# Scores of the first batch's chunks two ahead, with four unread products per chunk

## The chip, the cores and the metric

The kernel runs on one core of a Trainium2 chip. A core has five engines with instruction queues of their own that run in order: TensorE (PE, matrix products), VectorE (DVE), ScalarE (ACT), GpSimd (POOL) and SyncE (SP), which here issues nearly all DMA. The metric is device microseconds of one execution, given as the median of several; lower is better.

## The reference, cut to what matters

There are 4 batches, 8 heads, 768 tokens and a head size of 48. The first part is a recurrence with a complex decay in each of the 48 rows of a state of 48 x 48 per head:

```
a = (a_re, a_im) * min(|a|, 0.999) / (|a| + 1e-6)
for t in range(768):
    S = a[t][:, None] * S + outer(k[t], v[t])      # complex S
    y[t] = q[t] @ real(S)
```

Its output, as 768 x 384 per batch, goes through a Fourier transform over tokens and one over features, of which the real part is added to it (u = x + mixed), a normalisation, an MLP of 384 -> 1536 -> 384, a token mixing MLP of 768 -> 256 -> 768 and a second MLP, each added to its input. The weights come as 64-bit floats.

## The kernel before, in words

For each batch the program has a scan on DVE (line 312 for the first batch, 540 for the others), which makes decayed queries and keys for every token; a chunk stage (lines 739 to 832), in which the 768 tokens are worked in 8 chunks of 96; the Fourier stage with the normalisation (`stage2`, line 954); and the dense products (`mlp`, `tok1`, `tok2`). The dense part of a batch runs beside the scan of the next, but the first batch has nothing dense to run beside, so its scan, chunk stage and Fourier stage stand at the program's start, up to about 192 us.

A chunk c in the first batch:

- `ch_load(c)` has SP load V (line 741) and the decayed keys Kn (line 744); two buffers of each, so chunk c+2 loads when chunk c has been read.
- `ch_sc(c, half)` makes the scores of 4 heads (line 753, TensorE, four products into one of three PSUM buffers "s"), and DVE multiplies them with the causal mask (line 760) into SBUF.
- `ch_u(c)` makes the chunk's own state u(c) = keys x values (lines 768 and 769, 16 small products into a PSUM buffer "l", of which there are three). DVE adds the state T(c-1) that came in, giving Aa(c) (line 779), and multiplies by the chunk's decay: lines 785 and 786 on DVE, 787 on POOL (in chunk 0 on DVE), and their sum is T(c) (line 789). Each chunk needs the T of the chunk before.
- `ch_y(c)` adds two products in PSUM, masked scores x values (line 802) and queries x T(c-1) (line 808); ACT copies the sum to xT (line 810).

Between the chunks the first batch converts the 64-bit weights to pairs of 32-bit parts (`convert`, lines 180 to 207): SP loads a tile (line 185), ACT runs lines 191 and 192, DVE line 194, POOL line 196, DVE line 199, ACT line 205, POOL line 206, and SP writes the parts to memory (line 207). `tick` advances the tiles that are under way by one step per chunk and begins as many new ones as the table `CF` says.

`warm(n, x)` (line 305) issues n products into a fresh "l" buffer that nobody reads. `WC` (line 32) says how many follow each y(c) of the first batch: 10 after chunk 6 and 12 after chunk 7.

After the chunks, `stage2` adds and subtracts pieces of xT: lines 982 and 988, for s = 0 on DVE and for s = 1 on POOL in the first batch, then line 999 on DVE, products with the transform's matrices (lines 1022 and 1033), their sums and differences cb on POOL (lines 1070 and 1071), and line 1085 on DVE, which adds them to the input.

The order on each engine is worked out by a scheduler when the program is built, from priorities in program order and from its own timing of the program; so a changed program order changes the order of every queue in places.

Of the kernel before, what the change touches and what calls it, by code (L numbers as in the profile page):

```python
# [28 lines left out]
W0, WS = 2, 8  # L29
CF = (2, 2, 2, 2, 2, 0, 8, 0)  # L30
AN = (5, 6, 6, None)
WC = (0, 0, 0, 0, 0, 0, 10, 12)
WZ, CL = 0, 1
XL = (0,), (0, 1, 2, 3, 4, 5)
AH = 4
# [18 lines left out]
def attn_fft_mixer_kernel(ctx: ExitStack, tc: tile.TileContext, aL, xL, vL, wL, qN, kN, vN, arN, aiN,  # L54
# [37 lines left out]
    def alloc(tag, shape, dt=F32, name=None):  # L92
        n = 1
        for x in shape[1:]:
            n *= x
        t = pool.tile([128, SIZE[tag]], dt, tag=tag, bufs=BUFS[tag], name=name or tag)
        return shaped(t[0:shape[0], 0:n], shape)
# [3 lines left out]
    def palloc(tag, shape):  # L101
        n = 1
        for s in shape[1:]:
            n *= s
        t = psum.tile([128, 512], F32, tag=tag, bufs=PSB[tag], name=tag)
        v = t[0:shape[0], 0:n]
        if len(shape) == 3:
            v = v.rearrange("p (a b) -> p a b", b=shape[2])
        return v
# [120 lines left out]
    def tick(n, loads=False):  # L230

        keep, stream[0] = stream[0], BACK
        active[:] = [g for g in active if next(g, "end") != "end"]
        for _ in range(n):
            g = begin()
            next(g)
            if not loads:
                next(g)
            active.append(g)
        stream[0] = keep  # L240
# [64 lines left out]
    def warm(n, x):  # L305

        ps = palloc("l", [128, 512])
        for _ in range(n):
            te.matmul(out=ps[:, 0:x.shape[1]], lhsT=ident[0:x.shape[0], :], rhs=x)
# [391 lines left out]
    def stage1(b):  # L701
# [34 lines left out]
        st = {}  # L736
        PU = "l" if b == 0 else "s"

        def ch_load(c):
            v = alloc("P", [96, 384], name="V")  # L740
            sp.dma_start(out=v, in_=vL[b, c])
            kt = alloc("A", [96, 8, 128], name="Kn")
            for hf in range(2):
                sp.dma_start(out=kt[48 * hf:48 * hf + 48],
                             in_=knd[hf].rearrange("(h c) s f -> c s h f", c=8)[c])
            st[c] = dict(v=v, kt=kt)

        def ch_sc(c, half):
            ps = palloc("s", [96, 4, 96])
            Q, K = qk[0][:, 1], qk[0][:, 0]  # L750
            for j in range(4):
                hc = (half * 4 + j) * 8 + c
                te.matmul(out=ps[:, j, :], lhsT=K[:, hc, :], rhs=Q[:, hc, :])  # L753
            sc = alloc("e", [96, 4, 96], name="sc")
            mb = mask.unsqueeze(1).to_broadcast([96, 4, 96])
            if half and OFF[2] & (1 << b):
                se.copy(out=sc, in_=ps)
                ge.tensor_tensor(out=sc, in0=sc, in1=mb, op=ALU.mult)
            else:
                ve.tensor_tensor(out=sc, in0=ps, in1=mb, op=ALU.mult)  # L760
            st[c][f"sc{half}"] = sc

        def ch_u(c):
            d = st[c]
            ps = palloc(PU, [112, 8, 48])
            for h in range(8):
                vv = d["v"][:, h * 48:h * 48 + 48]
                te.matmul(out=ps[0:64, h, :], lhsT=d["kt"][:, h, 0:64], rhs=vv)  # L768
                te.matmul(out=ps[64:112, h, :], lhsT=d["kt"][:, h, 64:112], rhs=vv)
            g = gm[b % 2].rearrange("p k (h c) -> p k h c", c=8)[:, :, :, c:c + 1]  # L770

            def gb(k, lo, hi):
                return g[lo:hi, k].to_broadcast([hi - lo, 8, 48])

            def v8(ap):
                return ap.rearrange("p (h e) -> p h e", e=48)
            if c:
                a = alloc("e", [112, 384], name="Aa")
                ve.tensor_tensor(out=v8(a), in0=v8(st["T"]), in1=ps, op=ALU.add)  # L779
                a = v8(a)  # L780
            else:
                a = ps
            y = yc[c % 2]
            x = alloc("e", [112, 384], name="Xx")
            ve.tensor_tensor(out=v8(x), in0=a, in1=gb(0, 0, 112), op=ALU.mult)
            (ge if c and b else ve).tensor_tensor(out=v8(y)[0:48], in0=a[64:112], in1=gb(1, 64, 112), op=ALU.mult)  # L786
            st["yop"] = (ge if c else ve).tensor_tensor(out=v8(y)[64:112], in0=a[0:48], in1=gb(1, 0, 48), op=ALU.mult)
            T = alloc("e", [112, 384], name="T")
            st["op"] = ve.tensor_tensor(out=T, in0=x, in1=y, op=ALU.add)
            st["Tn"] = T  # L790
            if b == 0:
                tops.append(st["op"])

        def ch_y(c):
            d = st[c]
            Q = qk[0][:, 1]
            ps = palloc(PU, [112, 4, 96])
            for p in range(4):
                for k in range(2):
                    h = 2 * p + k  # L800
                    m = 48 if k else 64
                    te.matmul(out=ps[64 * k:64 * k + m, p, :], lhsT=d["v"][:, h * 48:h * 48 + m],  # L802
                              rhs=d[f"sc{h // 4}"][:, h % 4, :], start=True, stop=(c == 0))
                if c:
                    for k in range(2):
                        h = 2 * p + k
                        m = 48 if k else 64
                        te.matmul(out=ps[64 * k:64 * k + m, p, :], lhsT=st["T"][:, h * 48:h * 48 + m],  # L808
                                  rhs=Q[:, h * 8 + c, :], start=False, stop=True)
            marked(se.activation(out=xT[:, :, c * 96:c * 96 + 96], in_=ps, func=ACTF.Copy, scale=gate[0:112, b:b + 1]))  # L810

        if b == 0:
            tick(CF[0])
        st_g2()
        ch_load(0)
        ch_load(1)
        ch_sc(0, 0)
        ch_sc(0, 1)
        for c in range(8):
            if c < 7:  # L820
                ch_u(c)
                ch_sc(c + 1, 0)
                ch_sc(c + 1, 1)
            ch_y(c)
            if b == 0 and WC[c]:
                warm(WC[c], ident)
            st["T"] = st.get("Tn")
            if c < 6:
                ch_load(c + 2)
            if b == 0 and c < 7:  # L830
                rests[0], rests[1] = tops[c], st["yop"]
                tick(CF[c + 1], c == 5)
# [366 lines left out]
    def chain(b):  # L1199
        stage1(b)  # L1200
        return stage2(b)
# [145 lines left out]
```

## Time and profile before

| what | us |
|---|---|
| median of 3 runs | 1102.39 |
| lowest and highest run | 1101.18, 1103.57 |
| the profiled execution | 1103.4 |
| its span on the core | 1101.6 |
| TensorE busy | 985.5 (89%) |
| VectorE busy | 784.3 (71%) |
| ScalarE busy | 506.2 (46%) |
| GpSimd busy | 387.3 (35%) |

The shares are means over the whole span. The granted clock of TensorE has a mean of 0.955 of full speed. Where a row gives a matrix product of 32-bit floats, it counts two records per product: "x8" is four products.

### The profile page before, as it was taken

Reading aid. Unit: us, or ns where it says so; the run is one execution under the profiler, and the core shown is the slowest. Engines: PE = TensorE matmul, PEld = TensorE weight load, DVE = VectorE, ACT = ScalarE, POOL = GpSimd, SP = SyncE. Lnnn points to the kernel's source line nnn. Section 1 sums busy time; section 2 is a strip of 40 time slices with the busy share of each in tenths; the row PEclk is TensorE's granted clock in tenths of the full one; section 3 lists DMA queues with packets and bytes.
Section 4 is the critical chain, followed back from the end, with each engine's and each line's share of the span. In section 5 each row is a group of like instructions: output and inputs, shape, how many; then the busy total and the mean of one; then the engine's idle time right before and its main releaser. Section 6 shows DMA issues by size and latency. Waiting matters only on the chain.

```text
span 1101.6 us, 21033 instructions
## 1 busy us (share of the span) xinstructions
PE 985.5 (89%) x7314; PEld 923.1 (84%) x7314; DVE 784.3 (71%) x2115; ACT 506.2 (46%) x1393; POOL 387.3 (35%) x520
## 2 busy tenths in 40 slices
PE   1368887999889999799998999999986999999997
PEld 0237775989788888699998899999976999999997
DVE  6986987999999668999767879985555433433332
ACT  6753355777876225867423567751124112121111
POOL 6643985573576444223226312211432002000000
PEclk9987797999999998899998999999988999999999
DMA  6137954686758664355565336655412433443432
GB/s 215 45 82 179 293 176 154 209 283 194 231 179 278 194 178 135 99 168 185 179 160 172 112 112 193 205 161 146 139 48 66 151 115 129 158 151 130 165 101 74
DMA packets 101536, 174.65 MB, mean 159 GB/s; under 512 B 11056, under 2 KB 61104, under 8 KB 100912
## 3 DMA queue, kind: packets, MB, share of 16 engines
q1 hardware_dynamic: 101424, 173.24, 51.1%
q8 instruction: 60, 0.98, 0.4%
q14 instruction: 52, 0.43, 0.1%
HBM read 133.88 MB, written 39.32 MB: 157 GB/s over the span
## 4 chain that ended last, share of the span: by engine, by line
PE 65%; DVE 10%; DMA 2%; ACT 1%; issue 1%; POOL 1%; SPq 0%; POOLq 0%; DVEq 0%; ACTq 0%
PE l L942 24%; PE l L926 22%; PE s L753 3%; PE s L642 2%; PE s L1033 2%; PE s L1022 2%; PE s L802 2%; DMA cvt<-wL 2%; PE s L808 1%; PE s L1147 1%; DVE ws L982 1%; PE s L1165 1%; PE s L768 1%; DVE cvt L199 1%; PE s L906 1%
## 5 line engine op out<-in xcount | busy, mean ns | idle before, releaser
L942 PE MATMUL l<-w,h 128*128 128x384 f32 x1728 | 332.5, 345 | 12.1 <-DVE h L932 8.4
L926 PE MATMUL l<-th,w 128*128 128x384 f32 x1152 | 314.4, 342 | 5.1 <-DVE h L932 2.6
L942 PEld LDWEIGHTS l<-w,h 128*128 128x128 f32 x1728 | 304.4, 192 | 16.8 <-DVE h L932 11.6
L926 PEld LDWEIGHTS l<-th,w 128*128 128x128 f32 x1152 | 210.8, 190 | 9.1 <-DVE h L932 4.1
L930 ACT ACTIVATE h<-l 128x384 fp32r<-128x384 f32 x192 | 94.0, 490 | 225.3 <-PE l L926 224.8
L926 PE MATMUL l<-tl,w 128*128 128x384 f32 x576 | 195.3, 339 | 0.0
L932 DVE SCALAR_TENSOR_TENSOR h<-l,h 128x384 fp32r<-128x384 f32 x192 | 106.2, 553 | 88.3 <-ACT h L930 87.9
L945 DVE TENSOR_TENSOR u<-u,l 128x384 f32<-128x384 f32 x192 | 105.4, 550 | 76.0 <-PE l L942 75.1
L926 PEld LDWEIGHTS l<-tl,w 128*128 128x128 f32 x576 | 109.1, 189 | 0.4 <-issue 0.2
L196 POOL TENSOR_TENSOR cvt<-cvt 128x384 int32<-128x384 int32 x56 | 64.8, 1163 | 38.2 <-DVE cvt L194 9.4
L466 PE MATMUL s<-misc,y 128*112 128x128 f32 x96 | 22.1, 377 | 52.1 <-DVE y L444 48.6
L753 PE MATMUL s<-qkt 112*96 112x96 f32 x512 | 59.7, 267 | 8.0 <-DVE sc L760 7.9
L466 PEld LDWEIGHTS s<-misc,y 128*112 128x112 f32 x96 | 14.5, 181 | 61.9 <-issue 27.3
L753 PEld LDWEIGHTS s<-qkt 112*96 112x96 f32 x512 | 53.4, 177 | 11.1 <-DVE sc L760 8.7
L786 POOL TENSOR_TENSOR yc<-Aa,gm 48x384 f32<-48x384 f32 x18 | 21.0, 1165 | 100.8 <-DVE Aa L779 100.8
L206 POOL TENSOR_TENSOR w<-cvt,w 128x384 fp32r<-128x384 f32 x44 | 51.1, 1170 | 10.5 <-ACT w L205 7.0
L199 DVE SCALAR_TENSOR_TENSOR cvt<-cvt 128x384 int32<-128x384 int32 x56 | 48.8, 878 | 7.0 <-POOL cvt L196 6.8
L1132 POOL TENSOR_TENSOR xl<-u,xh 128x384 fp32r<-128x384 f32 x18 | 17.9, 1004 | 101.1 <-ACT xh L1131 101.1
L571 POOL TENSOR_TENSOR tm<-tm 128x144 f32<-128x144 f32 (+1 forms) x51 | 26.6, 523 | 73.7 <-ACT tm L570 73.7
L642 PE MATMUL s<-misc,y 128*112 128x128 f32 x288 | 45.7, 275 | 1.5 <-DVE y L626 1.0
L615 DVE TENSOR_TENSOR p<-p,A 128x144 f32<-128x144 f32 x144 | 44.7, 310 | 2.0
L589 POOL TENSOR_TENSOR A<-raw,tm 128x144 f32<-128x144 f32 (+1 forms) x51 | 26.1, 513 | 56.0 <-DVE tm L587 29.4
(232 smaller groups left out, 1905.3 us busy)
## 6 DMA issues: line engine op xcount, KB each, us to landing
w<-wscr SPq DMA_DIRECT2D x180, 384.0 KB, 3.5
cvt<-wL SPq DMA_DIRECT2D x56, 384.0 KB, 4.7
wscr<-w SPq DMA_DIRECT2D x44, 384.0 KB, 3.2
Kn<-kn SPq DMA_DIRECT2D x64, 192.0 KB, 3.8
kn<-y SPq DMA_DIRECT2D x96, 96.0 KB, 2.7
raw<-aL SPq DMA_DIRECT2D x48, 144.0 KB, 3.0
xx<-xL SPq DMA_DIRECT2D x48, 144.0 KB, 3.2
V<-vL SPq DMA_DIRECT2D x32, 144.0 KB, 3.3
```

The lines of the kernel that those rows point to most:

```text
L196: x = ge.tensor_tensor(out=a, in0=a, in1=lo, op=ALU.add)
L199: rest(ve.scalar_tensor_tensor(out=a, in0=hi, scalar=-0x80000000, in1=a, op0=ALU.bitwise_and, op1=ALU.bitwise_or))
L206: ge.tensor_tensor(out=parts[:, 1, :], in0=a.bitcast(F32), in1=r32(parts[:, 0, :]), op=ALU.subtract)
L466: te.transpose(ps[:, j, :], y[:, j, 0:112], ident)
L615: ve.tensor_tensor(out=cur, in0=prev, in1=A[:, j, 0:3, :], op=ALU.mult)
L642: te.transpose(ps[:, j, :], y[:, j, 0:112], ident)
L753: te.matmul(out=ps[:, j, :], lhsT=K[:, hc, :], rhs=Q[:, hc, :])
L926: te.matmul(out=ps, lhsT=w1[:, wi, kt * 128:kt * 128 + 128], rhs=x[g][:, kt, :], start=(n == 0), stop=(n == 8))
L930: x = se.activation(out=hi, in_=ps, func=ACTF.Relu)
L932: ve.scalar_tensor_tensor(out=h[:, 1, g * 384:g * 384 + 384], in0=ps, scalar=0.0, in1=r32(hi), op0=ALU.max, op1=ALU.subtract)
L942: te.matmul(out=ps, lhsT=hs[m][:, hi, tt * 128:tt * 128 + 128], rhs=w2[:, wi, :], start=(n == 0), stop=(n == 8))
L945: ve.tensor_tensor(out=u[tt], in0=u[tt], in1=ps, op=ALU.add)
```

## The change

`WC` gets 4 unread products after each of the chunks 0 to 5 of the first batch. The scores of the first batch are made and masked two chunks ahead instead of one: before the loop for chunks 0 and 1, and in round c for chunk c+2. As scores of a chunk can now come before its load, the chunk's dictionary is made by whoever comes first. The other batches stay one chunk ahead. The table of conversions `CF` is as before.

```diff
-WC = (0, 0, 0, 0, 0, 0, 10, 12)
+WC = (4, 4, 4, 4, 4, 4, 10, 12)
...
-            st[c] = dict(v=v, kt=kt)
+            st.setdefault(c, {}).update(v=v, kt=kt)
...
-            st[c][f"sc{half}"] = sc
+            st.setdefault(c, {})[f"sc{half}"] = sc
...
-        ch_sc(0, 0)
-        ch_sc(0, 1)
+        lead_sc = 2 if b == 0 else 1
+        for c in range(lead_sc):
+            ch_sc(c, 0)
+            ch_sc(c, 1)
         for c in range(8):
             if c < 7:
                 ch_u(c)
-                ch_sc(c + 1, 0)
-                ch_sc(c + 1, 1)
+            if c + lead_sc < 8:
+                ch_sc(c + lead_sc, 0)
+                ch_sc(c + lead_sc, 1)
             ch_y(c)
             if b == 0 and WC[c]:
                 warm(WC[c], ident)
```

Lines after 832 carry a number higher by 3 in the changed kernel: 982 is 985 there, 988 is 991, 1070 is 1073.

The first place is TensorE's queue in the middle of u(0), at the start of the chunk stage (lines 768 and 769 are u(0), 753 the scores):

```order
 L769 MATMUL l<-V,Kn 48x48
 L768 MATMUL l<-V,Kn 64x48
-L753 MATMUL s<-qkt 96x96 x4
+L753 MATMUL s<-qkt 96x96 x12
 L769 MATMUL l<-V,Kn 48x48
 L768 MATMUL l<-V,Kn 64x48
```

Where one half of chunk 0's scores stood, both halves of chunk 1 stand as well.

The second place is POOL's queue from the product of chunk 5 to the first sums of the Fourier stage (787 is a chunk's product, 196 and 206 are conversions, 982 and 988 pieces of the Fourier stage, 1070 and 1071 the sums cb). Before:

```order
L787 TENSOR_TENSOR yc_80<-Aa,gm_81 48x384
L196 TENSOR_TENSOR cvt<-cvt 128x384
L206 TENSOR_TENSOR w<-cvt,w 128x384 x2
L196 TENSOR_TENSOR cvt<-cvt 128x384
L982 TENSOR_TENSOR xf<-xT 112x4x96
L206 TENSOR_TENSOR cvt<-cvt 128x384
L787 TENSOR_TENSOR yc_79<-Aa,gm_81 48x384
L988 TENSOR_TENSOR xd<-xf 112x2x96 x2
L206 TENSOR_TENSOR cvt<-cvt 128x384
```

And in the changed kernel:

```order
L787 TENSOR_TENSOR yc_80<-Aa,gm_81 48x384
L196 TENSOR_TENSOR cvt<-cvt 128x384 x2
L985 TENSOR_TENSOR xf<-xT 112x4x96
L206 TENSOR_TENSOR cvt<-cvt 128x384
L991 TENSOR_TENSOR xd<-xf 112x2x96 x2
L206 TENSOR_TENSOR cvt<-cvt 128x384
L787 TENSOR_TENSOR yc_79<-Aa,gm_81 48x384
```

The product of chunk 6 has moved behind the two of line 988 and the conversion that followed it; two conversions of line 206 stand ahead of chunk 5's product now.

The third place is POOL's queue after the last pieces of the Fourier stage's input. Before:

```order
L196 TENSOR_TENSOR cvt<-cvt 128x384 x6
L206 TENSOR_TENSOR cvt<-cvt 128x384 x5
L196 TENSOR_TENSOR cvt<-cvt 128x384
L206 TENSOR_TENSOR cvt<-cvt 128x384
L196 TENSOR_TENSOR cvt<-cvt 128x384
L1070 TENSOR_TENSOR ws<-ws 128x193
```

And in the changed kernel:

```order
L196 TENSOR_TENSOR cvt<-cvt 128x384 x6
L206 TENSOR_TENSOR cvt<-cvt 128x384
L196 TENSOR_TENSOR cvt<-cvt 128x384
L206 TENSOR_TENSOR cvt<-cvt 128x384 x2
L196 TENSOR_TENSOR cvt<-cvt 128x384
L206 TENSOR_TENSOR cvt<-cvt 128x384 x4
L1073 TENSOR_TENSOR ws<-ws 128x193
```

Seven of line 206 stand ahead of the first sum where six stood; the eight of line 196 come earlier among them.

## Rows read from the trace of the kernel before

**Rows 1.** The page: busy us of each engine, and the end chain by engine.
```profile
PE 985.5 (89%) x7314; PEld 923.1 (84%) x7314; DVE 784.3 (71%) x2115; ACT 506.2 (46%) x1393; POOL 387.3 (35%) x520
...
PE 65%; DVE 10%; DMA 2%; ACT 1%; issue 1%; POOL 1%; SPq 0%; POOLq 0%; DVEq 0%; ACTq 0%
```

**Rows 2.** Busy time by stretch: from:to, length, busy of engines, clock, DMA.
```profile
84.00:97.00 13.00, 11.30 (x131) 10.37 (x131) 6.83 (x23) 2.13 (x9) 0.00 (x0) 0.56 0.45 95
97.00:152.00 55.00, 43.32 (x541) 39.00 (x540) 48.90 (x74) 24.20 (x55) 46.53 (x38) 0.83 0.93 285
152.00:170.50 18.50, 17.93 (x130) 15.14 (x128) 13.88 (x18) 8.32 (x21) 18.04 (x16) 0.96 0.33 129
```

**Rows 3.** DVE's timeline, T of chunks 0, 2, 6: start, us, what, idle before.
```profile
94.15 0.56 DVE L789 TENSOR_TENSOR T<-Xx,yc 112x384 f32<-112x384 f32 x1
...
107.28 0.56 DVE L789 TENSOR_TENSOR T<-Xx,yc 112x384 f32<-112x384 f32 x1 [0.74 <-POOL yc L787]
...
138.94 1.18 DVE L789 TENSOR_TENSOR T<-Xx,yc 112x384 f32<-112x384 f32 x1
```

**Rows 4.** DVE's waits from 84 to 152 us: total, times, longest.
```profile
DVE T L789 <- POOL yc L787: 2.5, 2, 1.8
...
DVE Aa L779 <- PE l L769: 0.9, 1, 0.9
```

**Rows 5.** Lines 786, 199 and 206 in the stage: ns minimum/median/maximum.
```profile
L786 DVE TENSOR_TENSOR yc<-Aa,gm x6: 1103/1270/1410, 98.3 to 137.4; 48x384 f32<-48x384 f32 x6
L786 DVE TENSOR_TENSOR yc<-l,gm x1: 559/559/559, 93.0 to 93.0; 48x384 f32<-48x384 f32 x1
...
L199 DVE SCALAR_TENSOR_TENSOR cvt<-cvt x10: 544/548/1361, 102.0 to 135.8; 128x384 int32<-128x384 int32 x10
...
L206 POOL TENSOR_TENSOR w<-cvt,w x8: 997/1310/3370, 104.8 to 130.1; 128x384 fp32r<-128x384 f32 x8
```

**Rows 6.** TensorE's timeline: scores in the opening and later, unread products.
```profile
89.95 1.60 PE L753 MATMUL s<-qkt 112*96 112x96 f32 x8
...
96.99 1.60 PE L753 MATMUL s<-qkt 112*96 112x96 f32 x16
...
141.49 1.61 PE L309 MATMUL l<-misc 128*128 128x128 f32 x12
```

**Rows 7.** Busy time and granted clock (third from the end) in the opening.
```profile
92.00:96.00 4.00, 4.00 (x43) 3.74 (x41) 3.66 (x9) 0.00 (x0) 0.00 (x0) 0.57 0.45 98
96.00:100.00 4.00, 4.00 (x89) 3.85 (x87) 2.84 (x5) 0.58 (x1) 2.12 (x2) 1.00 0.56 153
```

**Rows 8.** Timelines of DVE and POOL where both idle.
```profile
103.39 0.36 DVE L194 TENSOR_SCALAR cvt<-cvt 128x384 int32<-128x384 int32 x1 [0.87 <-ACT cvt L191]
...
104.75 1.38 POOL L206 TENSOR_TENSOR w<-cvt,w 128x384 fp32r<-128x384 f32 x1 [3.13 <-DVE Aa L779]
...
111.78 0.55 DVE L199 SCALAR_TENSOR_TENSOR cvt<-cvt 128x384 int32<-128x384 int32 x1
```

**Rows 9.** Timelines of POOL and DVE at the end of the chunk stage.
```profile
139.67 4.25 POOL L982 TENSOR_TENSOR xf<-xT 112x384 f32<-112x384 f32 x2
...
140.04 1.00 DVE L760 TENSOR_TENSOR sc<-s,misc 96x384 f32<-96x384 f32 x2
...
144.57 0.86 DVE L982 TENSOR_TENSOR xf<-xT 112x384 f32<-112x384 f32 x1 [1.51 <-ACT xT L810]
...
147.72 1.64 POOL L988 TENSOR_TENSOR xd<-xf 112x192 f32<-112x192 f32 x2
```

**Rows 10.** Timelines of POOL and DVE before the Fourier stage's sums.
```profile
167.32 0.99 POOL L206 TENSOR_TENSOR cvt<-cvt 128x384 fp32r<-128x384 f32 x1
...
169.56 0.52 POOL L1070 TENSOR_TENSOR ws<-ws 128x193 f32<-128x193 f32 x1
...
170.42 0.34 DVE L1085 TENSOR_TENSOR u<-s,ws 128x192 f32<-128x192 f32 x1
```

**Rows 11.** The chain that ended last, one of its pieces: start, us, what.
```profile
349.97 7.49 DMA cvt<-wL
```

## The prediction

> **What bounds the kernel now.** I read first the page's busy line and its end chain [rows 1]. Over the span TensorE is the busy engine (89%) and 65% of the chain is TensorE. But most of the span is the dense products, which the change leaves alone; what it does in the chunk stage of the first batch has to be read from that stage.
>
> So second the table by stage [rows 2]. The chunk stage has two parts. From 84 to 97 us POOL is idle, DVE half idle, and TensorE busy for 11.3 of 13 us: the opening is a TensorE stretch. From 97 to 152 us TensorE is busy for 43.3 of 55 us, DVE for 48.9 and POOL for 46.5. From 152 to 170.5 us POOL is busy for 18.0 of 18.5.
>
> Third the DVE timeline at the product T of each chunk (line 789), which the next chunk needs [rows 3]: T starts at 107.28 in chunk 2 and at 138.94 in chunk 6, so four chunks take 31.7 us, 7.9 each. What sets that pace? DVE waits for TensorE once after the opening, 0.9 us at Aa (line 779) of chunk 1, and twice, 2.5 us, for POOL [rows 4]; no later chunk waits for a score product or a y product. Instead the two engines lengthen each other. Line 786 takes 0.56 us in chunk 0, where POOL idles, and a median of 1.27 us in chunks 1 to 6; line 199 takes 0.55 at its shortest and 1.36 at its longest in the stage; line 206 takes 0.99 at 167.32, where DVE idles, and up to 3.37 in the stage [rows 5, 10]. Alone, a chunk's five POOL instructions would be some 5 x 1.0 = 5.0 us and DVE's work on SBUF operands 5 x 0.55 + 2 x 0.36 = 3.5 us; the sum, 8.5, is near the measured 7.9, the larger of the two is not. I therefore treat DVE and POOL as one resource from 97 us until line 1085 at 170.42, and ask when its work starts and how long both users stand idle at once.
>
> The Trainium skill has a rule for it (SBUF — State Buffer, section "SBUF: two separate sides"): DVE with two SBUF inputs and GpSimd take one port pair as an exclusive lock, and the later one blocks for the whole instruction. It speaks against this change, since by it a late start is not made up out of the idle time of either engine. The lengthened rows above agree.
>
> **The change, part by part.**
>
> *Opening.* TensorE's queue has three halves of scores (12 products) between the two parts of u(0) where there was one. At that place a half, 8 records, takes 1.60 us [rows 6], since the granted clock is at its lower level (0.57 over 92 to 96) [rows 7]; so the second part of u(0) comes 3.2 us later, and with it T(0), which started at 94.15. Of this, the scores of chunk 1 were TensorE's work before T(1) anyway. Counted up to the end of u(1), TensorE has this more to do: the scores of chunk 2, 16 records in 1.60 us, which run at the upper level, and four unread products at 1.61/6 = 0.27 each (12 records are 6 products), 1.07 together [rows 6]. The sum is 2.7, less some 0.1 of pipeline overlap, 2.6. Aa(1) waited for u(1) before (0.9 [rows 4]) and will again. DVE alone would be ready a little earlier: T(0) ends at about 97.9, two masks (1.0) and two of line 194 (0.7) follow, 99.6, against u(1) at some 99.7. So the term is **+2.6**. If the clock rose only after all of this, everything at the lower level would cost about 5.2; if it rose early enough to halve the two moved halves, 2.6 − 1.6 = 1.0. I take 2.6, because the rows put the rise at about 95, and TensorE's work before that is the same.
>
> *What the shared stretch absorbs.* Only time in which both engines idle can give the delay back. There is 0.87 us before line 194 at 103.39 (ACT waited for a weight load), about 0.5 until POOL's line 206 at 104.75, while DVE reads PSUM, and some 0.4 until line 199 at 111.78: 1.8 us [rows 8]. POOL's own 3.13 us before 104.75 is mostly DVE's working time. The weight loads that ACT waited for stand in SP's queue behind V, which waits for y(0), so they come later too, by 1.5 us or more. I take **−1.3**, between 0 and −1.8.
>
> *The middle chunks.* Masks and conversions are the same in number. The four unread products cost TensorE 1.07 us per chunk, twice that at the lower clock, and it has 11.7 us free between 97 and 152 [rows 2]. They take a third buffer of the PSUM ring of three, so y(c+1) now waits for ACT's copy of y(c), and u(c+1) for Aa(c). Behind a late y stand V, the next two weight loads and Kn in SP's queue, and behind those u, two chunks on. DVE's and POOL's 7.9 us per chunk cover this, and I cost it at 0; if the cover goes, a wait like the 0.9 us of Aa(1) appears.
>
> *T(6) and the tail.* On POOL the product of chunk 6 (line 787) now stands behind one more of line 206 and two of line 988: 0.99 + 1.64 = 2.6 us [rows 9, 10]. Against it, y(7) no longer waits for two masks behind T(6). T(6) ended at 140.1, and DVE's line 982 of the last piece started at 144.57, having waited 1.51 for ACT's copy of y(7) [rows 3, 9]; with 1.00 of masks and the 1.61 of unread products gone from between, these 4.4 us become about 1.9. The two cancel. Term **0**, from −1.0 (the masks) to +1.7 (POOL's transforms held up by DVE's for longer, as in the 4.25 us of two at 139.67).
>
> *Before cb(0).* POOL has seven of line 206 instead of six between line 982's last piece and line 1070, which releases line 1085: 0.99 us. Line 1085 started 0.34 after line 1070's end (169.56 + 0.52) [rows 10], behind a line 199 that is now earlier, so some 0.3 of it is hidden. Term **+0.7**, from 0 to 1.0.
>
> *After 192 us* the same work follows, with some loads and transposes in another order; cost 0, with a spread (a rival, below).
>
> Sum: +2.6 − 1.3 + 0 + 0.7 = **+2.0 us**. The profiled execution took 1103.4 us, its span of 1101.6 and 1.8 around it; it would take 1105.4. It lies 1.0 above the median of the runs, 1102.39 (1101.18 to 1103.57), so I predict **1104.4 us**. The ends of the terms add up to −1.8 (1.0 − 1.8 − 1.0 + 0) and +7.9 (5.2 + 0 + 1.7 + 1.0).
>
> **Rivals.**
>
> *Faster: DVE's chain sets the end, and the opening is swallowed.* If the two engines do not exclude each other as I read it, POOL's 3.13 us of idle time before 104.75 takes in the whole +2.6, and the end of the stage is DVE's chain, which loses the 1.51 us wait for ACT and the 1.00 of the last two masks: 1102.4 − 2.5 = 1099.9. For it: DVE's waits [rows 4, 9]. Against it: the lengthened rows [rows 5]. It decides if line 982 of the last piece, 144.57 before, starts by 142.1.
>
> *No change: the clock rises earlier.* With more products in a row in the opening, TensorE would reach the upper level sooner. Only the opening gains, since the later chunks do not wait for TensorE: the two moved halves at 0.80 (half of 16 records' 1.60) instead of 1.60, 1.6 less, so the sum is +0.4 and the time 1102.8. Against it: TensorE was already busy for 4.00 of 4 us between 92 and 96, and still at 0.57 [rows 7]. The Trainium skill (TensorE: Matmul & The Clock Gate, "Part 1: The HAM clock gate") has activity release the throttle, which would make this rival likelier.
>
> *The order after 192 us decides.* Weight loads stand on the end chain as pieces, one of 7.49 us [rows 11]. About half of such a piece more or less, 4 us, gives 1100.4 or 1108.4. For it: the orders of all engines differ in places up to the end. Against it: mostly neighbours have changed places.
>
> **How the numbers follow.** No change is what lies within 0.2% of 1102.4, that is 1100.2 to 1104.6, about what a measurement of this kernel can tell. My forecast has a chance of 0.60, with a spread of about 2 us around 1104.4: 0.30 slower, 0.30 no change. DVE's chain: 0.17, of which 0.13 faster and 0.04 no change. Earlier clock: 0.10, of which 0.08 no change and 0.02 slower. The order after 192: 0.13, of which 0.05 faster, 0.02 no change and 0.06 slower. Together 0.18 faster, 0.44 no change, 0.38 slower. The forecast's own range is 1102.0 to 1107.0; with the rivals, 1099.6 to 1107.6 leaves out about 0.2.
>
> **What would show it.** Right: Aa(1) at 99.4 to 100; chunks 2 to 6 still 7.6 us or more apart; line 786 still at a median of 1.27 us; line 1085 about 2 us after 170.42. Wrong: chunks closer than 7.4 us (then TensorE or its clock did count); Aa(1) before 98.5 (the clock); line 1085 at or before 170.4 (absorbed); or a stretch from line 1085 to the end that differs from 1101.6 − 170.4 = 931.2 us by over 2.

## The result, and the profile after

| what | before | after |
|---|---|---|
| median of 4 runs, us | 1102.91 | 1115.89 |
| lowest and highest run | 1101.18, 1103.57 | 1112.32, 1116.53 |
| the profiled execution's span | 1101.6 | 1114.7 |

The ratio is 1.0111 (95%: 1.0095 to 1.0126): slower by 12.2 us, where the forecast was 2.0 and its range ended at 1107.6. Below line 832 every line number of the changed kernel is 3 higher: L985 is line 982 before, L1088 is 1085.

The page of the changed kernel, busy us and the end chain by engine, answers to [rows 1]. TensorE has 3.4 us more work in a span that is 13.1 longer, and the chain leans more on DVE (16% for 10%):

```profile
PE 988.9 (89%) x7362; PEld 924.8 (83%) x7362; DVE 790.8 (71%) x2115; ACT 503.8 (45%) x1393; POOL 383.6 (34%) x520
...
PE 60%; DVE 16%; ACT 2%; issue 2%; POOL 1%; DMA 1%; POOLq 0%; DVEq 0%; ACTq 0%
```

The first batch's start, by stretch as in [rows 2] and [rows 7] (length, busy time of PE, PEld, DVE, ACT, POOL, granted clock, DMA):

```profile
84.00:97.00 13.00, 11.28 (x114) 10.40 (x115) 6.40 (x22) 1.66 (x8) 0.00 (x0) 0.60 0.38 82
97.00:152.00 55.00, 44.55 (x599) 39.08 (x597) 48.96 (x73) 24.58 (x50) 42.97 (x38) 0.91 0.91 276
92.00:96.00 4.00, 4.00 (x43) 3.77 (x42) 2.45 (x6) 0.00 (x0) 0.00 (x0) 0.70 0.05 11
```

DVE's timeline in the chunk stage, for [rows 3], [rows 9] and [rows 10]: start, us, what, idle before. T of chunk 0, Aa(1), T of chunks 2 and 5, two pieces of line 991, Aa(6), T of chunk 6, line 982's last piece, and line 1088, the first to read the Fourier stage's sums:

```profile
96.52 0.56 DVE L789 TENSOR_TENSOR T<-Xx,yc 112x384 f32<-112x384 f32 x1
99.28 0.55 DVE L779 TENSOR_TENSOR Aa<-T,l 112x384 f32<-112x384 f32 x1 [0.73 <-PE l L769]
...
109.16 0.56 DVE L789 TENSOR_TENSOR T<-Xx,yc 112x384 f32<-112x384 f32 x1 [0.74 <-POOL yc L787]
...
131.24 0.56 DVE L789 TENSOR_TENSOR T<-Xx,yc 112x384 f32<-112x384 f32 x1 [0.74 <-POOL yc L787]
...
135.87 3.33 DVE L991 TENSOR_TENSOR xd<-xf 112x192 f32<-112x192 f32 x2
139.12 0.54 DVE L779 TENSOR_TENSOR Aa<-T,l 112x384 f32<-112x384 f32 x1
...
141.48 1.18 DVE L789 TENSOR_TENSOR T<-Xx,yc 112x384 f32<-112x384 f32 x1
...
147.69 0.56 DVE L985 TENSOR_TENSOR xf<-xT 112x384 f32<-112x384 f32 x1 [0.62 <-ACT xT L810]
...
173.40 1.37 DVE L1088 TENSOR_TENSOR u<-s,ws 128x192 f32<-128x192 f32 x4 [3.28 <-POOL ws L1073]
```

Before, T(5) and Aa(6) stood here:

```profile
130.32 1.34 DVE L789 TENSOR_TENSOR T<-Xx,yc 112x384 f32<-112x384 f32 x1
...
133.72 0.54 DVE L779 TENSOR_TENSOR Aa<-T,l 112x384 f32<-112x384 f32 x1
```

T is 2.4 us late in chunk 0 (94.15), 1.9 in chunk 2 (107.28), 2.5 in chunk 6 (138.94); line 982's last piece is 3.1 late, L1088 3.0. From there to the end of the span it takes 1114.7 − 173.4 = 941.3 us, against 931.2 before: 10.1 of the 13.1 us arise after the part that the prediction worked out.

Line 786, which the prediction took as the sign that DVE and POOL lengthen each other, is as before or a little shorter (median 1.18 for 1.27 us) [rows 5]:

```profile
L786 DVE TENSOR_TENSOR yc<-Aa,gm x6: 1101/1180/1280, 100.4 to 140.3; 48x384 f32<-48x384 f32 x6
```

DVE's waits from 84 to 152 us answer to [rows 4]: at T 1.5 us for POOL, 0.7 for TensorE at Aa(1); after 100 us it waits for no product of TensorE at all, but at line 199 it waits 2.3 us for POOL, for 0.4 before:

```profile
DVE T L789 <- POOL yc L787: 1.5, 2, 0.7
...
DVE Aa L779 <- PE l L769: 0.7, 1, 0.7
```

TensorE's timeline answers to [rows 6]: three halves of scores in the opening, then four unread products. Then the piece that the prediction did not see: y(7) with the unread products of chunk 7 (24 records, 12 products) between its first four records and the rest:

```profile
89.97 4.16 PE L753 MATMUL s<-qkt 112*96 112x96 f32 x24
...
97.00 1.16 PE L309 MATMUL l<-misc 128*128 128x128 f32 x8
...
139.72 0.58 PE L802 MATMUL l<-sc,V 96*64 96x96 f32 x4 [4.06 <-DVE Aa L779]
140.23 5.48 PE L309 MATMUL l<-misc 128*128 128x128 f32 x24
145.64 0.38 PE L808 MATMUL l<-qkt,T 112*64 112x96 f32 x4
```

The clock in that stretch (length, busy time of TensorE alone, granted clock, DMA): TensorE is idle for 3.7 of 4 us, then runs at the lower level, and is back at the upper one in the course of the next four:

```profile
136.00:140.00 4.00, 0.28 (x4) 0.84 1.00 321
140.00:144.00 4.00, 4.00 (x21) 0.50 1.02 379
144.00:148.00 4.00, 3.02 (x37) 0.80 0.54 172
```

After 192 us, the busy time of TensorE alone by stretch (length, busy, granted clock, DMA), first before:

```profile
180.00:300.00 120.00, 110.08 (x617) 0.95 0.67 215
300.00:460.00 160.00, 144.55 (x1247) 0.95 0.57 176
...
800.00:860.00 60.00, 48.53 (x274) 0.86 0.22 69
sum 680.00, PE 639.77; mean PE 127.95
```

and after:

```profile
180.00:300.00 120.00, 106.93 (x607) 0.96 0.64 208
300.00:460.00 160.00, 140.87 (x1234) 0.97 0.58 178
...
800.00:860.00 60.00, 45.16 (x297) 0.83 0.14 49
sum 680.00, PE 629.71; mean PE 125.94
```

The sums are of 180 to 860. TensorE's idle time there is 680 − 639.77 = 40.2 us before and 680 − 629.71 = 50.3 after. From 860 to 1060 it is busy throughout in both. So in these two profiles the engine that bounds the dense part waits 10.1 us more, about as much as is lost after L1088. Its longest waits from 192 us to the end, after (total, times, longest):

```profile
PE s L909 <- ACT ws L1115: 14.4, 5, 5.7
PE l L945 <- DVE u L948: 6.2, 5, 2.5
PE s L1025 <- ACT ws L1009: 5.8, 1, 5.8
```

and before:

```profile
PE s L906 <- ACT ws L1112: 12.1, 4, 5.7
...
PE l L942 <- DVE u L945: 3.4, 1, 3.4
```

The wait in the Fourier stage (L1025, which was 1022) did not exist before. Against that, the waits of lines 926 and 942 for line 932 (929, 945 and 935 after) fell from 11.0 to 7.3 us. The three loads of weights that stood among the longest pieces of the end chain, of 4.65 to 7.49 us [rows 11], are not among them any more.

### The profile page after: what moved, and what is told of

Read it like the earlier page. It is cut to its first block, busy times and chain, and to the rows that moved or that the text cites. A ratio compares the mean times of both kernels' runs of the same rounds, so it can differ in the third digit from the quotient of the medians.

```text
span 1114.7 us, 21133 instructions
## 1 busy us (share of the span) xinstructions
PE 988.9 (89%) x7362; PEld 924.8 (83%) x7362; DVE 790.8 (71%) x2115; ACT 503.8 (45%) x1393; POOL 383.6 (34%) x520
## 4 chain that ended last, share of the span: by engine, by line
PE 60%; DVE 16%; ACT 2%; issue 2%; POOL 1%; DMA 1%; POOLq 0%; DVEq 0%; ACTq 0%
PE l L929 22%; PE l L945 20%; PE s L753 3%; PE s L642 2%; DVE cvt L199 2%; PE s L1025 2%; PE s L1036 2%; PE s L802 2%; DVE u L948 2%; DVE ws L991 1%; PE s L808 1%; PE s L1150 1%; DVE ws L985 1%; PE s L1168 1%; PE s L768 1%
## 5 line engine op out<-in xcount | busy, mean ns | idle before, releaser
L945 PE MATMUL l<-w,h 128*128 128x384 f32 x1728 | 325.7, 340 | 10.8 <-DVE u L948 6.2
L945 PEld LDWEIGHTS l<-w,h 128*128 128x128 f32 x1728 | 299.6, 189 | 16.0 <-DVE u L948 8.5
L206 POOL TENSOR_TENSOR w<-cvt,w 128x384 fp32r<-128x384 f32 x44 | 48.8, 1116 | 11.2 <-ACT w L205 9.5
```

Of the source, the lines that this page charges most:

```text
L206: ge.tensor_tensor(out=parts[:, 1, :], in0=a.bitcast(F32), in1=r32(parts[:, 0, :]), op=ALU.subtract)
L945: te.matmul(out=ps, lhsT=hs[m][:, hi, tt * 128:tt * 128 + 128], rhs=w2[:, wi, :], start=(n == 0), stop=(n == 8))
```

## The experiments

In all that follows a ratio is to the kernel before, run on the same chip in the same rounds, with its 95% interval; us are the ratio less one, times 1103.

**Start and order apart.** From the load of smat (line 962) to the end both kernels issue the same 9342 instructions; only their order on the engines differs. All kernels below but b_lead_alone and b_products_alone hold each engine's queue in a recorded order, with edges that set an order and add no wait (the recorded lists make the line numbers of these kernels higher):

```diff
+    made = [i for i in nc.cur_bb.bb.instructions[first[0]:] if "Tile" not in type(i).__name__]
+    for d in steps:                       # one list per engine
+        at += d
+        if prev is not None:
+            tc.add_manual_dep(made[at], made[prev].name, HOLD, reason="order kept")
+        prev = at
```

The changed start with the old order:

> The changed kernel, but from the Fourier stage of batch 0 (the load of smat) to the end every engine's queue is held in the order of the kernel before; only the first chunk stage is the changed one. The profiles put L1085 about 3 us later after the change and the end 13 later. Theory A (the order of the queues after 192 us costs the other 8 to 10): 3 to 5 us over the kernel before, 1105.5 to 1108, and the shift of batches 1 to 3 stays at what it is at the first dense product. Theory B (a late first stage costs more downstream by itself, whatever the order): 1112 or more, with the shift growing through batches 1 to 3 as in the changed kernel. The forecast of the prediction, which costed the order at nothing: 1104.4.

1.0031 (1.0015 to 1.0046): +3.4 us, as theory A had it. The old start with the new order:

> The other half: the kernel before, with every engine's queue from the load of smat to the end held in the order of the changed kernel. Theory A: 7 to 10 us slower than the kernel before (1110 to 1113), with L1085 at its old 170.4. Theory B: within 2 us of 1102.9. If the two halves add up, their sum is about 13 us; if both come out under 5, the order only fits its own start and the cost is in the pair (theory C).

1.0123 (1.0103 to 1.0144): +13.6 us, with not an instruction added, and more than the 7 to 10 of theory A. Its account holds and B falls: in the profile of the changed start with the old order the shift of the dense products stays at 4.1 to 4.4 us from 379 us to the end. The sum, 17, is over the 12.2 of the whole: on the changed start the new order costs 12.2 − 3.4 = 8.8 us, on the old one 13.6, so a start and its own order fit each other better. TensorE's busy time over 180 to 860 goes with the order, not with the start (sums of the same view, the changed start with the old order, then the old start with the new one):

```profile
sum 680.00, PE 638.49; mean PE 127.70
```

```profile
sum 680.00, PE 629.86; mean PE 125.97
```

Idle time is not all of it. The profiled execution of the old start with the new order was the shortest of five: 1110.73 us at a mean granted clock of 0.964, with a span 7.4 us over the kernel before. The other four took 1115.91 to 1118.18 us at 0.944 to 0.953. So part of the 13.6 us comes with a lower clock, and no profile of such an execution of this kernel was kept.

**Which half of the change.** With the old order held, the lead alone and the unread products alone:

```diff
-WC = (4, 4, 4, 4, 4, 4, 10, 12)
+WC = (0, 0, 0, 0, 0, 0, 10, 12)          # lead alone
-        lead_sc = 2 if b == 0 else 1
+        lead_sc = 1                      # products alone
```

> Only the lead of two (no unread products in chunks 0 to 5), the rest from the load of smat on in the order of the kernel before. By the prediction's terms the lead is the scores of chunk 2 in the opening (+1.6), less what the both-idle stretches absorb (1.3): +0 to +1, 1103 to 1104. Rival: the lead makes the whole of the first stage's 3 us (1105.5 to 1108), or brings time (DVE's chain, under 1102).

1.0009 (0.9997 to 1.0021): no difference that can be told. DVE's rows for T(1) and T(6) in its profile:

```profile
101.11 1.20 DVE L870 TENSOR_TENSOR T<-Xx,yc 112x384 f32<-112x384 f32 x1
...
138.95 1.18 DVE L870 TENSOR_TENSOR T<-Xx,yc 112x384 f32<-112x384 f32 x1
```

Against the profile of the kernel before (99.55 and 138.94) T(1) is 1.6 us late, as the term for the scores of chunk 2 said, and T(6) not at all. But the same chunk stage does not start at the same time in every execution: in the nine profiles that have it unchanged T(6) stands at 137.56 to 138.94, and that of the kernel before is the latest. Against their means (99.61 and 138.23) T(1) is 1.5 us late and T(6) 0.7, so that the stage gives back about half.

> Only the four unread products per chunk (scores one chunk ahead as before), the rest from the load of smat on in the order of the kernel before. By the prediction's terms 1.07 in the opening, absorbed, and one more L206 on POOL before cb: 0 to +0.7, 1102.5 to 1103.5. Rival: the unread products, not the lead, make the first stage's 3 us, through POOL's order and the ring of three PSUM buffers (1105.5 to 1108).

1.0029 (1.0019 to 1.0040): +3.2 us. The rival was right: of the changed start's 3.4 us the unread products make nearly all; what the lead makes cannot be told from nothing. In this profile DVE waits 3.70 us for ACT's copy of y(7), and the first line 1085 stands at 173.46.

The same two in the scheduler's own order:

> The changed kernel without the unread products of chunks 0 to 5: the lead of two alone, in whatever order the scheduler then gives. 816 of TensorE's 5411 places after the load of smat differ from the kernel before, but the number of dense products that stand ahead of each step of the chain stays within 6 of what it was (in the changed kernel 10 to 29 more stand ahead of the steps of batches 2 and 3). If what costs is dense products moved ahead of the chain (theory A): as with the old order, 1103 to 1105. If any reshuffle of the order costs (theory D): 1107 or more.

1.0053 (1.0040 to 1.0067): +5.8, so theory D. The count of dense products ahead of the chain is no measure of the cost: it was as before to within 6, and the order alone cost some 5 us. TensorE's idle time over 180 to 860 goes with the cost here: 42.0 us with the old order, 47.0 in this one.

> The four unread products per chunk alone, lead of one, in the scheduler's own order: 15 to 31 more dense products stand ahead of the chain's steps in batches 2 and 3, much as in the changed kernel. Theory A: 3 us in the first stage and the order's 8 to 13 on top, 1111 to 1117. If the lead and the products are both needed for the loss: under 1108.

1.0163 (1.0149 to 1.0177): +18.0, a little above what was expected. The idle time is 49.4 us, no more than in the changed kernel at +12.2; but the granted clock was 0.50 from 168 to 200, through the end of the Fourier stage and the first dense products.

**Where in the order.** The two orders agree at many places as to which instructions have gone, so a queue can change from one to the other there:

> The kernel before, its queues held in the changed kernel's order from the load of smat to about 405 us (the middle of batch 1's chunk stage), and in its own order from there. Up to there few dense products stand further ahead (0 to 9). Theory A by the count: 1 to 5 us over the kernel before. By the profile of the run with the whole new order, which was 3.9 us late at 403 of 7.7 at the end: about half of that run's 13, 5 to 7.

1.0041 (1.0026 to 1.0056): +4.5.

> The other half: its own order to about 405 us, then the changed kernel's, where 18 to 27 more dense products stand ahead of the chain of batch 2 and 21 ahead of batch 3's chunks. Theory A by the count: the larger part, 6 to 10 us over the kernel before, with the new wait of 5.8 us for the copies at line 1006 (L1009 after the change) in batch 3's Fourier stage.

1.0039 (1.0026 to 1.0053): +4.3. Neither half has "the larger part", and together they make 8.8 of 13.6: the loss is spread, and by these ratios the rest is in the pair. The wait in batch 3's Fourier stage came as expected.

**Single places.** Two were tried. In batch 0's Fourier stage the new order puts the last two of 16 unread products ahead of the waits that they filled; near 810 us it puts a group of nine dense products ahead of batch 3's first products of line 1022, and has fewer of them left there. On TensorE, line by line with the number of products, as the traces have them (a product of line 942 is one record, of the others two):

```
before: 309 x5, 1022 x4, 309, 1022 x4, 1033 x4, 309, 1080
after:  309 x7, 1022 x8 (as L1025), 1033 x4 (as L1036), 1080 (as L1083)
before: 942 x45, 1022 x12, 942 x9, 1022 x20
after:  942 x33 (as L945), 1022 x32 (as L1025)
```

The first was undone in two kernels that have the new order:

> The kernel before with the whole order of the changed kernel from the load of smat on, except for 14 places on TensorE in batch 0's Fourier stage: there the last two of its 16 unread products stand again behind the next group of line 1022 and behind the first of line 1033, where they fill waits for the copies of line 1024, instead of all ahead of them. With the whole new order TensorE was idle for 2.2 and 0.7 us there, and the lower clock from about 162 to 196 was seen in one profile of such an order (b_new_to_400_then_old) and not in another (a_old_start_new_order). Theory F (those two waits let the clock fall in most executions, and that is 5 to 6 of the order's 13 us): 1109 to 1112 and a narrow spread. Otherwise 1115 to 1117 as with the whole order.

1.0090 (1.0067 to 1.0114).

> The changed kernel with its own order, except for the same 14 places on TensorE. Its profile shows the granted clock at 0.50 to 0.68 over 168 to 180. Theory F: L1036's 16 products of 6.5 us fall to 3.8 and the whole from 1115.9 to 1111 to 1113. Otherwise 1115 to 1117.

1.0087 (1.0069 to 1.0105). Both are some 3 us better than the kernels that they were made from (1.0123, 1.0111), the second as theory F had it and the first nearly so, but the intervals overlap and they come from other rounds. Done alone in the kernel before, it does nothing, and theory F falls as the swap's own price:

> The kernel before and its order, with one swap: the last two unread products of batch 0's Fourier stage stand ahead of the groups of line 1022 and 1033 instead of behind them (14 of 5411 places). Theory F: TensorE idle some 2 us more over 158 to 166, the lower clock over part of 160 to 196 in some executions, 2 to 4 us slower with a wider spread. If the loss needs the rest of the new order: within 1 us of before.

1.0001 (0.9991 to 1.0011). Nor does the other:

> The kernel before and its order, with one swap near 810 us: one group of nine dense products of line 942 stands ahead of batch 3's first 12 products of line 1022 instead of behind them (21 of 5411 places). TensorE should then wait about 5.8 us for line 1006's copies with nothing in between, and line 1022's 64 records run at the lower clock (11.4 us in the changed kernel's order against 7.0). By the profiles' step between 791 and 821: 1.3 to 1.6 us slower. If the clock alone counted: 4. If the dense products lost there are made up later: within 0.5.

1.0001 (0.9986 to 1.0015). Here the step of 1.3 to 1.6 us was expected and did not come: in the old order 54 dense products in a row (27 before the wait of 3.42 us, 27 behind it) still cover the wait for line 1006's copies (L1023 is line 942, L1103 line 1022):

```profile
803.42 7.86 PE L1023 MATMUL l<-w,h 128*128 128x384 f32 x27 [3.42 <-DVE u L1026]
811.12 6.81 PE L1103 MATMUL s<-dcos,ws 112*128 112x97 f32 x64
```

The rows of TensorE's timeline show what differs in the new one. Before:

```profile
803.08 6.03 PE L942 MATMUL l<-w,h 128*128 128x384 f32 x18 [3.42 <-DVE u L945]
808.94 2.82 PE L1022 MATMUL s<-dcos,ws 112*128 112x97 f32 x24
811.54 1.81 PE L942 MATMUL l<-w,h 128*128 128x384 f32 x9
813.19 4.13 PE L1022 MATMUL s<-dcos,ws 112*128 112x97 f32 x40
```

The changed kernel:

```profile
810.97 1.86 PE L945 MATMUL l<-w,h 128*128 128x384 f32 x9 [0.59 <-DVE u L948]
818.67 11.43 PE L1025 MATMUL s<-dcos,ws 112*128 112x97 f32 x64 [5.85 <-ACT ws L1009]
```

Of its dense products only 33 are left there, TensorE stands for 5.85 us, and 64 records that took 2.82 + 4.13 us take 11.43.

**The unread products in the middle of y(7).** The changed start, the old order, and one edge that puts chunk 7's unread products behind y(7):

```diff
-                warm(WC[c], ident)
+                warm(WC[c], ident, st["ym"] if c == 7 else None)   # behind y(7)'s last product
```

> As a_new_start_old_order (the changed first stage, the old order from smat on; 1107.5), but the unread products of chunk 7 stand behind all products of y(7) instead of in the middle of them, where 24 records took 5.5 us at the lower clock. Theory G (that is the 3 us of the first stage that the prediction put at 0): ACT's copy of y(7) about 4 us earlier, L1085 back to 170 to 171, 1103.5 to 1105. Rival (DVE and POOL set the end of the stage anyway): L1085 within 0.5 of that run's, 1106.5 to 1108.

1.0005 (0.9996 to 1.0014), against 1.0031 without the edge: the changed start's cost can no longer be told from nothing. But the way is not the one that theory G named. L1085 (L1171 here) starts at 171.11, and in the profile without the edge at 171.19, no later. The difference comes behind it: the granted clock from 172, without the edge

```profile
172.00:176.00 4.00, 3.90 (x14) 0.50 0.41 159
```

and with it

```profile
172.00:176.00 4.00, 3.98 (x24) 1.00 0.43 168
```

Without it line 1085 of the third block of tokens starts 1.4 us later (179.13 for 177.74), and at 416 us the dense products are 4.35 us behind the kernel before, with it 0.82. One profile each; that the place of the 12 products decides is shown by the ratios, that it decides through the clock from 172 us on is not.

**Three places together.** The edge of y(7) and both swaps undone, in the changed kernel with its own order:

> The changed kernel with its own order, but for three places on TensorE: the unread products of chunk 7 behind y(7); the last two unread products of batch 0's Fourier stage where they were before; and in batch 3's Fourier stage one group of nine dense products again behind the first 12 products of line 1022 (L1025 after the change). If three places add up: 1115.9 less 3.1, less 3.0, less some 1.5, 1107 to 1109. If the loss is in these three alone: 1104 to 1105. If undoing single places gains nothing since the next wait takes over: 1112 or more.

1.0161 (1.0137 to 1.0185): +17.8, worse than the changed kernel. Of the three theories only the last is left ("1112 or more"), and it did not say worse. The profile says where: the clock was 0.50 from 168 to 200, and in batch 3's Fourier stage the nine dense products put back found the dense queue empty around them, with a wait of 8.27 us ahead of the first 24 records of line 1022 (L1109 here):

```profile
818.78 5.43 PE L1109 MATMUL s<-dcos,ws 112*128 112x97 f32 x24 [8.27 <-ACT ws L1093]
823.92 3.23 PE L1029 MATMUL l<-w,h 128*128 128x384 f32 x9
828.82 7.07 PE L1109 MATMUL s<-dcos,ws 112*128 112x97 f32 x40 [1.67 <-DVE ws L1086]
```

The edge of y(7), which gained 2.9 us with the old order, was not tried alone in the new one. What is right in one order can be wrong in another.

**A faster version.** If waits and the clock behind them are what costs, the kernel before can have unread products put into its own waits, with its order held:

> A try at a faster version: the kernel before with its order, and 12 unread products after the first and 12 after the fourth group of transposes of line 906 in batch 0, where TensorE waits 2.7 and 2.5 us and its clock is at 0.50 to 0.67 from 176 to 192. If the clock holds at 1.00: the nine transposes 1 us shorter and the first dense products (L926 from 186.2) at full speed, 1 to 3 us faster than the kernel before, 1100.5 to 1102.5. If the waits set the start of the dense products anyway and the clock falls behind the fill: no change; if the fill itself runs at the lower clock, up to 1 us slower.

0.9997 (0.9986 to 1.0008): no change. The clock held until 184 and fell in the next wait.

```diff
+FILL = ((0, 12), (3, 12)), ((1, 22), (3, 5)), 13   # batch 0's transposes, batch 3's, 799.7 us
+            x = te.matmul(out=ps[:, 0:128], lhsT=ident, rhs=ident)
```

> A try at a faster version by the same reason: the kernel before with its order and unread products put into five of TensorE's waits: 12 and 12 between batch 0's transposes of line 906, 13 into the wait of 3.4 us at 799.7, 22 and 5 between batch 3's transposes (waits of 5.7 and 1.5 us). If the clock holds at 1.00 there: 18 dense products at 803 take 3.4 instead of 6.0 us, and after 836 the transposes and first dense products gain about 2.3: 3 to 5 us faster, 1099 to 1101. If the waits' ends set the time and not the products: no change. If the fill delays what it stands ahead of: 1 to 2 us slower.

0.9985 (0.9972 to 0.9999): 1.7 us faster than the kernel before, less than the 3 to 5 expected and just outside the interval of no change, and some 14 us less than the changed kernel by the two ratios. The first dense products at 803 run at full speed (18 records in 2 x 1.84 for 6.03 us), but the next wait took over part of it (L984 are the unread products, L1042 is line 942):

```profile
800.08 3.06 PE L984 MATMUL s<-misc 128*128 128x128 f32 x26
803.67 1.84 PE L1042 MATMUL l<-w,h 128*128 128x384 f32 x9 [0.53 <-DVE u L1045]
806.15 1.84 PE L1042 MATMUL l<-w,h 128*128 128x384 f32 x9 [0.65 <-DVE u L1045]
```

## Why the prediction was wrong

The step that failed is *After 192 us*, "the same work follows, with some loads and transposes in another order; cost 0, with a spread". The same work does follow, and its order alone makes the time 1.0123 of what it was on the old start (+13.6 us), and costs 8.8 us on the changed one. The rival for it stood there with a chance of 0.13, but was priced from the wrong thing: half of one piece of the chain of waits [rows 11], 4 us of either sign. What the order sets is how long TensorE, 89% busy, has nothing to do over 680 us, which rose from 40.2 to 50.3, and in some executions at what clock it runs. Its reason against, "mostly neighbours have changed places", is true of four engines, whose instructions that changed place moved by 1 to 3 places in the mean, and not of TensorE: between the two recorded lists 2283 of its 5410 instructions (the expectations count 5411) changed place, by 15 places in the mean and by up to 80. Nor are small moves safe: the lead alone left the dense products where they were, to within 6 by count, and its order still cost some 5 us.

The other steps, by the profiles of the kernel before and the changed one, and where it matters by the means of the nine profiles with the old chunk stage and the five with the whole changed one, since the same stage starts earlier or later in other executions, by over 1 us:

- *Opening*, +2.6. T(0) +2.4 and Aa(1) +2.2 (99.28 against 97.11), a little under the 99.4 that was to show it; by the means Aa(1) is +1.8. The three halves took 4.16 us instead of 4.8, and the clock was at 0.70 over 92 to 96, for 0.57, so it rose somewhat earlier, as the second rival had it in part. Right in kind, and a little too large.
- *What the shared stretch absorbs*, −1.3. From T(1) (+2.1) to T(5) (+0.9) it gave back 1.2; by the means 0.6, inside the step's bounds. So the agreement to 0.1 is luck. By the Trainium skill (SBUF — State Buffer, section "SBUF: two separate sides") DVE and POOL hold a port pair in turn; line 786's 1.18 us beside a busy POOL, against 0.56 in chunk 0, agrees again, and it was not what failed. Line 786 of chunk 0 reads u(0) from PSUM, however, and is not quite the same instruction; line 789 is, and takes 0.56 in chunks 0, 2 and 5, where DVE waited for POOL's product or POOL was idle, and 1.18 or 1.19 in the others.
- *The middle chunks*, 0. Chunks 2 to 6 took 32.3 us, 8.1 each, for 7.9. But up to T(5) they took 7.4 each, for 7.7, and the last one 10.2, which belongs to the next step. The 7.4 touch what was to be a sign that TensorE counts; but after 100 us DVE waits for no product, and what became less is its wait for POOL at T (1.5 us for 2.5). Right.
- *T(6) and the tail*, 0, from −1.0 to +1.7. From T(5) (+0.9) to line 982's last piece (+3.1): +2.2. Failed, by the engine that it looked at. It priced POOL's queue at 2.6 us, but POOL's product of chunk 6 waited for Aa(6) (0.82 us). What moved is DVE's queue: Aa(6) stands behind both pieces of line 991, 3.33 us beside a busy POOL, and starts 7.9 us after T(5), for 3.4; from there to T(6) it is 2.4, for 5.2. Together T(5) to T(6) takes 10.24 us for 8.62. It takes 10.22 to 10.24 in every profile with the unread products in chunks 0 to 5, and 8.61 or 8.62 in every one without: these 1.6 us are theirs.
- *The tail behind T(6)*, of the same step. From T(6) to line 982's last piece it is 6.2 us for 5.6. The step let the masks and "the 1.61 of unread products gone from between" shorten this by 2.5. The masks are gone, but DVE's pieces of lines 985 and 991 now take 4.5 us for 2.1; and the unread products were not gone: 24 records of them took 5.48 us inside y(7) at a clock of 0.50 for the most part, after TensorE had been idle for 4.06 us. The price of an unread product had been taken from a row at the upper level. Of these 5.48 us DVE felt only the wait of 0.62 for the copy of y(7); with the edge, in c_products_behind_y7, that wait is gone and the stretch still takes 6.3.
- *Before cb(0)*, +0.7. From line 982's last piece to L1088 the shift went from 3.1 to 3.0: 25.7 us for 25.9. Two effects cancel here. On the old start with the new order the same stretch takes 26.8: the order, with its seventh line 206, costs 0.95 of the 0.99 that the step reckoned. With the old order on the changed start it takes 24.7.
- *The sum at L1088*: +2.0 forecast, +3.0 measured: opening some 0.5 too large, tail 2.2 too small, cb 0.8 too large. That the changed start costs +3.4 us by itself, inside the forecast's own range, is in part luck: with the old order line 1085 comes 0.8 us late, and the rest arises behind it, up to 379 us.
- *The rivals*. DVE's chain was to decide if line 982's last piece started by 142.1; it started at 147.69. The earlier clock came in part, worth some tenths.

The clock gate was weighed in the opening alone. The Trainium skill (TensorE: Matmul & The Clock Gate, "Part 1: The HAM clock gate") has the clock follow TensorE's activity; the rows agree at the places shown here: 0.28 of 4 us busy over 136 to 140 and 0.50 over the next four, 5.85 us idle near 813 and 11.43 us for 64 records behind it. Applied to the end of the stage it would have priced the unread products there at the lower level.

What stays open: which places of the new order make its 10 us or more. Two single swaps make none of it in the old order, either half of the order makes 4, and three repairs together made it worse. It is spread, and the places lean on each other. Open too: how the 13.6 us divide between idle time and a lower clock.

## What to carry to other kernels

Where a scheduler orders the queues by its own timing, an edit at the front is two edits: what it does where it stands, and a new order everywhere behind it. Hold the order behind the edit to price the first, and hold the new order on the old front to price the second; here they were +3.4 and +13.6 us. The lists of the two orders say how far the second has moved; "mostly neighbours" should be counted, engine by engine. Products that nobody reads can be held by an edge behind the product that somebody waits for, since a scheduler may put them ahead of it: with the old order that edge took the time from 1.0031 to 1.0005, while in the new order, with two other places, it did not help. And where one profile is compared with another, stretches between two instructions tell more than the times at which they start: T(5) to T(6) repeats to 0.02 us, T(6) itself to 1.4.

## What the runs showed of the hardware

- Unread products took 1.61 us per 12 records at the upper level [rows 6]; the 24 that began after 4.06 us of idle time took 5.48, 1.7 times as much, at a granted clock of 0.50 over 140 to 144 and 0.80 over 144 to 148. Here the fill paid the lower level itself, and the upper one came back in its last part or just behind it.
- Filling waits lifted the mean granted clock of the whole kernel from 0.955 to 0.967 in the profile of d_before_filled, and the time fell by 0.15% only. TensorE's waits here end with another engine's work, as in the rows at 803.67 and 806.15; that this is why so little came of it was not tested.
- On the old start with the new order the five executions took 1110.73 us at a mean granted clock of 0.964 and 1115.91 to 1118.18 at 0.944 to 0.953: one kernel, one order, and 7 us between them.
